# Regrouping TensorE's attention work and sharing half of w_in between two batches, in an attention and MLP kernel on one core

## The chip, the cores and the metric

The kernel runs on one core of a Trainium2 chip. The metric is the device time of one execution in microseconds (us), as the median of several executions. Before the change it is 1549.52 us (three runs, 1549.14 to 1550.99). The profiled execution: its span, from the first to the last instruction, is 1543.8. Profiles are used only to see where time goes.

Engines: TensorE (PE: matmuls; PEld: its weight loads), VectorE (DVE), ScalarE (ACT), GpSimd (POOL), SyncE (SP, which issues transfers). The granted clock is the share of TensorE's full clock that the profile shows for a stretch. A matmul of the program shows as two instructions in the profile, a transpose as one; each is called a pass here, and the counts (x8) are passes. An eviction is the instruction that takes a finished product out of its PSUM bank.

## The reference, cut to what matters

```python
# attention: batch 8, heads 12, sequence 448, head_dim 64, float32
q_n, k_n = rmsnorm(q, g_q), rmsnorm(k, g_k)       # x / sqrt(mean(x*x) + 1e-6) * g
attn = softmax(q_n @ k_n.T / 8)
x = (attn @ v).transpose(0, 2, 1, 3).reshape(3584, 768)
# then an MLP; w_in and w_out arrive as float64
h = x @ w_in                                       # 768 x 2048
out = (h * sigmoid(h)) @ w_out                     # 2048 x 768
```

## The kernel before

Attention goes by pairs of heads: 6 pairs a batch, 48 in all, numbered n. The keys' positions are cut into four chunks j of 112. The parts that matter, with cuts marked:

```python
def normalise(n):                    # two pairs ahead
    # ... cut: squares on ScalarE, sums and scaling on VectorE, power -0.5 on GpSimd
    for i, name in enumerate("qk"):
        # ... cut: factor = rms of this name
        nc.gpsimd.tensor_tensor(out=normal[name]..., in0=st[name], in1=factor..., op=ALU.mult)

def transpose(n, name):              # 4 TensorE transposes into the one bank "tr"
    # ... cut
    if name == "q":
        nc.scalar.copy(features[name], t)
    else:
        nc.vector.tensor_scalar_mul(out=features[name], in0=t, scalar1=gains)

def scores(half):                    # two chunks of keys, both heads: contraction over 64 rows
    for j in range(2 * half, 2 * half + 2):
        # ... cut: two matmuls into banks[:, h, :]
        nc.scalar.activation(e[j], banks[:, :, 0:S], AF.Exp)      # both heads at once

def weigh(n, half): ...              # "av": weights times values, 64 output columns
def add_up(half): ...                # VectorE: sums of the chunks' exps
def unload(n): ...                   # ScalarE: copy of av out of its bank
def divide(n):                       # "ones": sums of exp on TensorE, 64 output columns
    # ... cut
    nc.vector.reciprocal(out=r, in_=t)
    nc.vector.tensor_tensor(out=xT(*pairs[n]), in0=xU, in1=r, op=ALU.mult)
```

The MLP's products are work that TensorE does between the parts of attention. Two batches are a group, and a block of 256 of w_in's columns times the group takes seven products of half-size blocks (Strassen's way) instead of eight, with sums of blocks made on VectorE beforehand. In the first two batches the weights are still arriving, so batch 0 is multiplied plainly (`whole(0)`) and batch 1 in seven products on halves of its own 448 tokens, 224 columns each.

```python
for n, (b, hp) in enumerate(pairs):
    load(n + 2)
    scores(0)
    fill()                               # a quarter of the MLP work due in this pair
    if n > 0:
        divide(n - 1)
        # ... cut: beginning of the next group's products
    weigh(n, 0); scores(1); add_up(0)
    # ... cut: rounding of w_in (batch 1)
    fill()
    transpose(n + 1, "q"); weigh(n, 1); unload(n); add_up(1)
    # ... cut: rounding of w_in (batch 1); sums of w_in's blocks (batch 2)
    fill()
    transpose(n + 1, "k"); normalise(n + 2)
    # ... cut: rounding of w_in; end of a group: the rest of its products, sums of x
    fill()
divide(last)
# ... cut
for _ in halves_in(group, prepare_out):  # the last group, with nothing of attention beside it;
    pass                                 # prepare_out fetches hidden, opens and rounds w_out
# ... cut: the output stage, 14 products-of-seven over w_out
```

"Rounding" turns the float64 weights into float32 in steps: a load, an opening on ScalarE, then three instructions on VectorE and one on GpSimd.

## Time and profile before

The table reads TensorE's timeline at the sums of exp ("ones") of a pair, which come once a pair and so serve as marks. Work given in the second column lies between two marks.

| from the sums of pair | what runs | us | length |
|---|---|---|---|
| start to 0 | loads, first norms, first pair | 0 to 31.45 | 31.45 |
| 0 to 5 | batch 0: attention alone, rounding of w_in | to 92.36 | 60.9 |
| 5 to 23 | batches 1 to 3: attention and the first group's products | to 416.05 | 323.7 |
| 23 to 35 | batches 4 and 5, beside group 2 | to 653.61 | 237.6 |
| 35 to 47 | batches 6 and 7, beside group 3 | to 887.76 | 234.2 |
| 47 to end | last group, output stage | to 1543.8 | 656.0 |

One more view bears on the shared half of w_in: the list of what TensorE waited for between 246 and 400 us (engine, line, releaser: us in all, times, longest).

```profile
PE mm L434 <- DVE stage L408: 13.9, 9, 2.0
```

Nearly all of the 15.5 us of waiting in that stretch is for one kind of VectorE instruction, the eviction of a half-width product.

### The profile page before, as it was taken

Reading aid. Unit: us, or ns where it says so; the run is one execution under the profiler, and the core shown is the slowest. Engines: PE = TensorE matmul, PEld = TensorE weight load, DVE = VectorE, ACT = ScalarE, POOL = GpSimd, SP = SyncE. Lnnn points to the kernel's source line nnn. Section 1 sums busy time; section 2 is a strip of 40 time slices with the busy share of each in tenths; the row PEclk is TensorE's granted clock in tenths of the full one; section 3 lists DMA queues with packets and bytes.
Section 4 is the critical chain, followed back from the end, with each engine's and each line's share of the span. In section 5 each row is a group of like instructions: output and inputs, shape, how many; then the busy total and the mean of one; then the engine's idle time right before and its main releaser. Section 6 shows DMA issues by size and latency. Waiting matters only on the chain. (4 is left out here: it accounts for less than half of the span.)

```text
span 1543.8 us, 14413 instructions
## 1 busy us (share of the span) xinstructions
PE 1464.2 (95%) x5216; PEld 743.5 (48%) x5216; DVE 759.0 (49%) x970; ACT 525.3 (34%) x744; POOL 408.7 (26%) x300
## 2 busy tenths in 40 slices
PE   5789999899899999999999989999999999999998
PEld 2234444555444444344444344445555555555554
DVE  4988876655765555665555575662121112121221
ACT  4558865555544544544444423420000000000000
POOL 4555533333333323332333223330000000000000
PEclk9999999999899999999999999999999999999999
DMA  6344221121211211311131064442222222222220
GB/s 194 96 128 144 72 78 55 60 61 60 72 60 48 85 59 42 103 60 60 42 102 42 27 212 131 155 149 76 75 75 75 75 75 75 75 75 86 75 85 23
DMA packets 87924, 128.96 MB, mean 84 GB/s; under 512 B 5924, under 2 KB 70948, under 8 KB 87844
## 3 DMA queue, kind: packets, MB, share of 16 engines
q1 hardware_dynamic: 87520, 127.95, 26.5%
q8 instruction: 43, 0.70, 0.2%
q14 instruction: 37, 0.30, 0.1%
q10 hardware_dynamic: 324, 0.00, 0.0%
HBM read 87.56 MB, written 40.37 MB: 83 GB/s over the span
## 5 line engine op out<-in xcount | busy, mean ns | idle before, releaser
L434 PE MATMUL mm<-x,W 128*128 128x448 f32 (+1 forms) x768 | 283.4, 507 | 14.7 <-DVE stage L408 13.1
L335 POOL TENSOR_TENSOR rms<-rms,minus_half 112x16 f32<-112x16 f32 x48 | 141.0, 2937 | 408.4 <-DVE rms L332 394.9
L368 ACT ACTIVATE work<-sc 112x896 f32<-112x896 f32 x192 | 166.1, 914 | 203.3 <-PE sc L365 203.0
L434 PE MATMUL mm<-sums_x,W 128*128 128x448 f32 (+1 forms) x576 | 210.9, 500 | 14.7 <-DVE parts L408 9.3
L434 PEld LDWEIGHTS mm<-x,W 128*128 128x128 f32 x768 | 141.1, 192 | 148.6 <-issue 122.8
L446 POOL TENSOR_TENSOR parts<-parts 128x448 f32<-128x448 f32 (+2 forms) x46 | 49.2, 1069 | 582.1 <-DVE parts L408 581.8
L434 PE MATMUL mm<-W,work 128*128 128x384 f32 x588 | 197.6, 486 | 0.0
L365 PE MATMUL sc<-work 64*112 64x448 f32 x768 | 175.4, 577 | 17.8 <-DVE work L358 17.8
L399 DVE RECIPROCAL work<-tr 128x448 f32<-128x448 f32 x48 | 141.8, 2953 | 88.7 <-PE tr L398 88.7
L408 DVE TENSOR_TENSOR stage<-mm,parts 128x448 f32<-128x448 f32 (+2 forms) x121 | 67.7, 562 | 237.5 <-PE mm L434 101.2
L408 DVE TENSOR_TENSOR parts<-mm,parts 128x448 f32<-128x448 f32 (+2 forms) x92 | 51.6, 561 | 265.7 <-PE mm L434 256.5
L388 DVE TENSOR_TENSOR work<-work 112x896 f32<-112x896 f32 x144 | 169.0, 1174 | 12.1 <-ACT work L368 5.5
L377 PE MATMUL av<-work,rows 112*64 112x448 f32 x768 | 165.3, 552 | 3.6 <-ACT work L368 3.6
L434 PEld LDWEIGHTS mm<-sums_x,W 128*128 128x128 f32 x576 | 104.5, 190 | 105.6 <-issue 79.5
L434 PEld LDWEIGHTS mm<-W,work 128*128 128x128 f32 x588 | 111.7, 190 | 77.9
L365 PEld LDWEIGHTS sc<-work 64*112 64x112 f32 x768 | 62.4, 176 | 115.7 <-issue 63.8
L441 ACT COPY parts<-mm 128x448 f32<-128x448 f32 (+2 forms) x46 | 21.8, 474 | 268.9 <-PE mm L434 268.9
L434 PE MATMUL mm<-W,x 128*128 128x384 f32 x336 | 112.9, 486 | 0.0
L340 POOL TENSOR_TENSOR work<-rows,rms 112x512 f32<-112x512 f32 x96 | 100.6, 1069 | 3.8
L444 ACT COPY parts<-mm 128x448 f32<-128x448 f32 (+2 forms) x46 | 22.1, 481 | 221.9 <-PE mm L434 221.9
L377 PEld LDWEIGHTS av<-work,rows 112*64 112x64 f32 x768 | 50.6, 138 | 82.3 <-issue 53.5
L434 PEld LDWEIGHTS mm<-W,x 128*128 128x128 f32 x336 | 63.8, 190 | 44.5
(66 smaller groups left out, 1437.4 us busy)
## 6 DMA issues: line engine op xcount, KB each, us to landing
hidden<-stage SPq DMA_DIRECT2D x48, 448.0 KB, 2.5
work<-hidden SPq DMA_DIRECT2D x7, 2048.0 KB, 9.0
x<-hidden SPq DMA_DIRECT2D x7, 2048.0 KB, 9.0
W<-in_moe_w_in_dram SPq DMA_DIRECT2D x24, 512.0 KB, 4.1
rows<-in_moe_w_out_dram SPq DMA_DIRECT2D x32, 384.0 KB, 3.1
rows<-in_q_dram SPq DMA_DIRECT2D x48, 224.0 KB, 3.6
rows<-in_k_dram SPq DMA_DIRECT2D x48, 224.0 KB, 3.8
rows<-in_v_dram SPq DMA_DIRECT2D x48, 224.0 KB, 3.6
```

The costliest lines, as they stand in the source:

```text
L335: nc.gpsimd.tensor_tensor(out=flat, in0=flat, in1=minus_half[0:R].to_broadcast([R, 4 * J]), op=ALU.pow)
L340: nc.gpsimd.tensor_tensor(out=normal[name].rearrange("p j h d -> p h j d"), in0=st[name], in1=factor.to_broadcast([R, 2, J, D]), op=ALU.mult,)
L365: nc.tensor.matmul(banks[:, h, 0:S], kT[rows, ts(j, R)], qT[rows, :], start=True, stop=True)
L368: nc.scalar.activation(e[j], banks[:, :, 0:S], AF.Exp)
L377: nc.tensor.matmul(st["av"][ds(h * D, D), :], st["v"][:, h, j, :], e[j][:, h, :], start=(j == 0), stop=(j == J - 1),)
L388: nc.vector.tensor_tensor(out=es, in0=e[0] if j == 1 else es, in1=e[j], op=ALU.add)
L399: nc.vector.reciprocal(out=r, in_=t)
L408: nc.vector.tensor_tensor(out=out, in0=a, in1=b, op=ALU.add)
L434: nc.tensor.matmul(t, left(name, s), right(name, s), start=i == 0, stop=i == len(steps) - 1)
L441: nc.scalar.copy(p1, (yield from product("1")))
L444: nc.scalar.copy(p5, (yield from product("5")))
L446: nc.gpsimd.tensor_tensor(out=u2, in0=u2, in1=p5, op=ALU.add)
```

## The change

Its intent: (1) TensorE goes to attention twice a pair instead of four times. One visit is scores, av, transpose; the other is sums of exp, scores, av, transpose; a longer fill follows each. VectorE's other work (rounding, sums of weights) is dealt out between these points in single steps. (2) The keys aren't multiplied by their norm any more. They are transposed raw, and their factor is the scale operand of exp, which then has to be one instruction per head. (3) Half of w_in is multiplied plainly with batches 0 and 1, the other half with both as one group, so the half-width products vanish. (4) Small things at both ends: the first pair's norms go ahead, six matmuls of a new group go ahead of the last sums of the old one, the last group begins beside the last pair, and the last store is split.

```diff
+def normalise_rows(nc, z, rows, normal, squares, rms, minus_half, engine):
+    # ... cut: squares, sums, power as before; only q is multiplied, on `engine`
     # transpose(n, "k"), cut:
+            rows = state[n]["k"].rearrange("p h j d -> p j h d")
+            if n < 2 * z.NPAIR:
+                nc.scalar.activation(kT, t, AF.Copy, scale=gains)
+            else:
+                nc.vector.tensor_scalar_mul(out=kT, in0=t, scalar1=gains)
     # scores, cut:
-            nc.scalar.activation(e[j], banks[:, :, 0:S], AF.Exp)
+            for h in range(2):
+                nc.scalar.activation(
+                    e[j][:, h, :], banks[:, h, 0:S], AF.Exp, scale=rms[n % 4][:, 1, h, j : j + 1]
+                )
     # products of the first two batches:
     def first_two():
-        yield from whole(0)
+        yield from whole(1, early)
         for c in range(HW):
-            sum_x([1], c)
-        yield from halves_in([1])
+            sum_x([0, 1], c)
+        yield from halves_in([0, 1], late)
     # the loop, cut to its order:
+    for n in range(last + 2):
+        load(n + 3, "qk")
+        if n <= last:
+            scores(n, 0)
+        if n > 0:
+            weigh(n - 1, 1)
+            load(n + 1, "v")
+            add_up(2, 3)
+            unload(n - 1)
+        transpose(n + 1, "q")
+        if n == 0:
+            normalise(2)
+        if ends:
+            begin(halves_in([b - 2, b - 1], range(HF), prepare_out if b == z.B else plain),
+                  products, 4 * NPAIR - 1)
+        weights_in(n, 0)
+        fill(2 * HW if ends else None)
+        weights_in(n, 1)
+        if n > 0:
+            divide(n - 1)
+        if n <= last:
+            scores(n, 1)
+            weigh(n, 0)
+        transpose(n + 1, "k")
+        if n <= last:
+            add_up(1)
+        # ... cut: sums of x; at n = 6 and 12 the first products begin
+        weights_in(n, 2)
+        # ... cut: at a group's end, the rest of its products
+            fill()
+        weights_in(n, 3)
+        normalise(n + 3)
```

Further cuts: the loads of w_in keep a list of which raw buffer each needs and go as early as that is free; keys are loaded in another order of rows ("p j h d"); rings of buffers are dealt anew.

## The prediction

> **What bounds the kernel now.** I read part 1 of the page first, then the table of stages (TensorE's busy time in chosen stretches), the chain that ended last, and TensorE's timeline where the stretches show idle time.
>
> ```profile
> PE 1464.2 (95%) x5216; PEld 743.5 (48%) x5216; DVE 759.0 (49%) x970; ACT 525.3 (34%) x744; POOL 408.7 (26%) x300
> ```
>
> TensorE is busy for 1464 of 1543.8 us, every other engine for half the span or less. A gain can come only from less TensorE work or from its 80 idle microseconds. The stretches (start:end, length, TensorE busy, its instructions, granted clock, DMA share, GB/s) say where those are:
>
> ```profile
> 18.00:90.00 72.00, 56.96 (x260) 0.95 0.37 103
> ...
> 246.00:400.00 154.00, 138.49 (x684) 0.99 0.20 60
> ...
> 460.00:650.00 190.00, 186.69 (x693) 1.00 0.19 61
> ...
> 880.00:926.00 46.00, 39.03 (x108) 0.93 0.56 180
> 926.00:1029.00 103.00, 95.51 (x252) 1.00 0.41 134
> 1029.00:1544.00 515.00, 508.20 (x1574) 1.00 0.25 77
> ```
>
> Idle: about 16 us before the first scores at 18.6, 15.0 in batch 0 (attention with nothing to fill in), 15.5 while batch 1's products run on half-width operands, 3.3 in 190 us of the steady stage, 14.5 around the last group of two batches, 6.8 in the output stage, nearly all of it after the last matmul. The output stage isn't changed but for its last store, so a third of the span is fixed. Now one steady pair, in the chain (start, us, what, instructions):
>
> ```profile
> 785.68 1.65 PE av L377 x8
> 787.34 3.20 PE mm L434 x8
> 790.54 0.39 PE tr L354 x4
> 790.92 3.02 PE mm L434 x8
> 793.95 1.69 PE sc L365 x8
> 795.64 2.45 PE mm L434 x6
> 798.09 0.90 PE tr L398 x4
> 798.99 1.50 PE av L377 x8
> 800.50 1.69 PE sc L365 x8
> 802.19 3.20 PE mm L434 x8
> 805.39 0.39 PE tr L354 x4
> ```
>
> TensorE is never without work here, so only its own cost counts. Attention is 1.65+0.39+1.69+0.90+1.50+1.69+0.39 = 8.21 us. The four fills hold 30 passes (a matmul is two) in 11.87 us. In the last group the chain shows 25.09 us for 66 passes without a break, 0.380 each, so 30 should take 11.40: going in and out costs 0.47 us a pair. A fill of eight after av or sc takes 3.20, after a transpose 3.02; av after a transpose takes 1.65, after other matmuls 1.50.
>
> The half-width stage repeats this:
>
> ```profile
> 310.54 1.40 PE L434 MATMUL mm<-x,W 128*128 128x224 f32 x6
> 313.59 1.02 PE L434 MATMUL mm<-x,W 128*128 128x224 f32 x4 [1.65 <-DVE stage L408]
> ```
>
> Three products of 224 columns are over before VectorE has emptied the bank that the next needs.
>
> **What the Trainium skill says.** "TensorE: Matmul & The Clock Gate", section "HAM oscillation — how this bites in real kernels", warns of idle gaps over about 3.4 us, after which matmuls run at half clock. The trace agrees, even for shorter pauses: after the 2.39 us wait at 885.4 the next 12 passes take 7.16 us, where 12 later ones take 4.67. So the pauses between groups cost more than their length. "ScalarE: Activation LUTs", "What ACT_TABLE_LOAD costs", gives 1283 ns a load; the trace has 1283. "Perfetto Trace Analysis", "Optimizing Scalar/DVE Operations", says that each instruction carries a fixed access overhead, so that larger ones pay: the exp of 896 elements takes 914 ns, a copy of 448 out of PSUM 530, so two halves cost some 146 ns more than the whole. "DMA: Bandwidth & Descriptors", "Why small descriptors are slow (HBM only)", bears on the keys' new layout, whose rows are 256 B instead of 1 KB; no trace of before shows such a load. As keys are fetched three pairs ahead, I count nothing for it.
>
> **The change part by part.** I count to the last attention matmul (885.4 us now), then the rest.
>
> *Two visits.* Order per pair: scores, av, transpose, fill; sums of exp, scores, av, transpose, fill. Both fills follow a transpose (no entry cost seen), and both avs follow scores (1.50): attention 8.06, and 0.62 us less a pair. Fills run beside 42 pairs (batches 1 to 7): 42 x 0.62 = **-26 us**, all of it on the path.
>
> *Half of w_in shared.* Before, 168 half-width matmuls; after, 84 full ones: the same columns. Their 15.5 us of idle time should go, since a full product lasts 6 x 0.38 = 2.28 us against an eviction of 0.62. It is counted with the waits below.
>
> *Start.* The first pair's norms go ahead of the branch, and its keys are transposed without waiting for them. gains still waits for its DMA until 7.0; two reductions (0.67 each), the power (2.9 on GpSimd), the multiply on VectorE (about 0.7), transposes (0.98) and a copy (0.53) put the first scores at about 14.4 instead of 18.6. But the second pair's squares now stand behind that copy, and its query passes power and multiply again (15.3 to 20.6), so that the sums of exp of pair 0 come at about 31.7, as now (31.45).
>
> *Batch 0.* VectorE decides: it waits for sums of exp that wait for its own additions. A round after: reciprocal 2.95, multiply 0.65, three additions of 1.17, three rounding steps 1.5, reductions and scaling 1.45, and about 1.1 for TensorE's sums in between: 11.15 us. Now the sums of pairs 0 to 5 stand at 31.45 and 92.36, 12.2 apart. The keys' factor for the first two batches goes to ScalarE, and fewer waits lie in the round. Pair 5's sums at about 31.7 + 5 x 11.15 = 87.5: **-5 us**.
>
> *The other waits up to 885.4.* From pair 5's sums on, work now is 42 x 8.21 - 2 + 96 x 0.76 + 168 x 0.38 + 336 x 0.76 + 42 x 0.47 = 755 us; the trace takes 793, so 38 are waits and half-clock time: 15.5 above, about 5 at each change of group (402 to 416 and 641 to 655, idle plus slow clock), 4.4 between 90 and 210, the rest small. After, I allow 20: 2.5 at pair 12, whose first fill is empty; 3.5 at each of two changes of group (six matmuls go ahead, but the third product waits for the last sums of x); 2 in batch 1, where ScalarE needs about 13 of 14.9 us a pair; 0.2 a pair for the key transpose, which now stands 3.19 us of TensorE work (1.69+1.50) behind the sums, just as long as the reciprocal holds the bank (2.95 plus hand-over). **-18 us**.
>
> *The end.* Before the last group the first w_out tile still lands some 9.6 us after its load, and ScalarE's copies stand behind it; and the order of rounding and evictions on VectorE is unchanged, so the four waits of about 2.4 us stay. I give 1.5 for the overlap and 0.5 for the split last store: **-2 us**.
>
> *More work elsewhere.* ScalarE gets 192 x 0.146 = 28 us of exps, GpSimd loses 48 x 1.07 = 51. Neither is on the path.
>
> Sum: -26 - 5 - 18 - 2 = -51, so a span near 1493. The three timed runs are 5.7 us over the profiled span (1549.5 against 1543.8); with that, 1498.
>
> **The rivals.** (1) *The key transpose becomes a wait in every pair.* For it: there is no slack, and an eviction ahead of the reciprocal in VectorE's queue (0.62 us, or a wait for GpSimd's addition) passes on whole. Against: VectorE is busy about 60% of a pair, and the 5.5 us fill ahead gives it time. At 0.8 us a pair, 42 x 0.6 = 25 us are lost: 1523. (2) *ScalarE becomes the bound in batches 1 and 2*: smaller exps, table loads around every silu and two openings of w_in a pair fill 87% of the shorter pair. At 2 us a pair over 9 pairs: 1514. (3) *Everything goes well*: no wait at the transpose, 224-column stage and changes of group clean, the loads of the last group no longer seen: 12 to 20 us better, 1480. (4) *The saved time is taken elsewhere*, because TensorE's first matmuls after attention cost the same wherever they stand: half of the 26 us fails, 1511.
>
> **Range and chances.** All rivals but a combination stay ahead of 1518.5, the 2% line. The work taken away (26) and the half-width waits are read from traces directly; the 20 us of new waits is the weak term and could double. Hence 1498, 1477 to 1523; faster 0.86, within 2% 0.12, slower 0.02.
>
> **What would show it.** A steady pair in the chain should show two fills of about 14 or 16 passes, about 5.5 us each, and a period near 8.06 + 14.6 x 0.76 = 19.2 us instead of 20.1 to 20.85. The list of waits should show TensorE's transposes behind the reciprocal for under 15 us in all; over 30 means rival 1. Exp groups: 384 of about 530 ns. Pair 5's sums near 87.5, the stretch between 246 and 400 over 96% busy, and the last group's first products still pausing for w_out. The prediction is wrong if TensorE idles behind ScalarE in batches 1 to 3, or if fills keep their entry cost.

## The result and the profile after

The changed kernel takes 1541.99 us (median of four runs, 1540.31 to 1543.97) against 1549.33 us (four runs, 1547.24 to 1550.99). Executions over 1.5% slower than the fastest of the same kernel are left out of the means. Ratios here are the mean time of one kernel's runs over the mean of the other's runs of the same rounds, so not quite the ratio of the medians quoted: 0.9954, with a 95% interval of 0.9936 to 0.9972. That is "the same" at 2%, and 44 us above the prediction. Of these 44, 3.9 come from the way in which the prediction turned its span into a time: it added 5.7 us to its span, the distance from the profiled span to the median of other, slower executions. An execution's time is only 1.8 us over its own span, before (1545.57 and 1543.8) and after (1541.16 and 1539.4). For the same reason the spans differ by 4.4 us and the medians by 7.3.

The first line of the page, busy time by engine:

```profile
PE 1460.6 (95%) x5048; PEld 706.8 (46%) x5048; DVE 739.7 (48%) x939; ACT 562.9 (37%) x928; POOL 379.9 (25%) x243
```

TensorE's busy time fell by 3.6 us where 26 were to go, and its idle time is unchanged: 1539.4 - 1460.6 = 78.8 us, before 1543.8 - 1464.2 = 79.6. The stretches, placed at the same stages as those of before (start:end, length, TensorE busy, its instructions, granted clock, DMA share, GB/s):

```profile
14.00:90.00 76.00, 58.66 (x271) 0.96 0.44 122
240.00:400.00 160.00, 154.67 (x594) 1.00 0.22 67
444.00:638.00 194.00, 191.88 (x720) 1.00 0.23 68
863.00:912.00 49.00, 35.00 (x86) 0.79 0.49 161
912.00:1023.00 111.00, 99.63 (x256) 0.97 0.40 128
```

The stretch from 240 to 400 is now 97% busy, before 90%. But the beginning of the last group is idle for 14.0 of 49 us at a granted clock of 0.79, where it was idle for 7.0 of 46 at 0.93, and the rest of that group is idle for 11.4 us of 111, before 7.5 of 103. By the same marks as above:

| sums of pair | before | after | length before | length after |
|---|---|---|---|---|
| 0 | 31.45 | 34.91 | 31.45 | 34.91 |
| 5 | 92.36 | 91.85 | 60.9 | 56.9 |
| 23 | 416.05 | 401.32 | 323.7 | 309.5 |
| 35 | 653.61 | 637.51 | 237.6 | 236.2 |
| 47 | 887.76 | 871.18 | 234.2 | 233.7 |
| end | 1543.8 | 1539.4 | 656.0 | 668.2 |

From pair 23 on the marks of after have six matmuls (4.5 us) of the next group ahead of them. So the stage from 5 to 23 gained 18.7 us, the two steady stages almost nothing, and the end lost 16.7.

A steady pair in the chain that ended last (start, us, what, instructions):

```profile
437.18 1.65 PE av L412 x8
438.83 0.53 PE tr L377 x4
439.37 5.28 PE mm L472 x14
444.64 0.90 PE tr L433 x4
445.55 1.69 PE sc L396 x8
447.24 1.65 PE av L412 x8
448.89 0.53 PE tr L382 x4
449.43 5.28 PE mm L472 x14
454.70 1.69 PE sc L396 x8
```

(L433 is the sums of exp.) The shape is as intended: two visits, two fills of 14 passes without a wait. The pieces aren't: both transposes take 0.53 us instead of 0.39, and both avs 1.65. Attention costs 0.90 + 2 x 1.69 + 2 x 1.65 + 2 x 0.53 = 8.64 us a pair. Before it was 8.21, and 0.47 more in the fills, 8.68. The fills themselves are clean now, 5.28 / 14 = 0.377 a pass. The mean period from pair 24 to 34 is 19.76 us; 19.2 was predicted. Before it was 20.39 over the same pairs, but this is no gain of 0.6 a pair: the work of a group is spread otherwise over its pairs, and the whole stage from pair 23 to 35 is only 1.4 us shorter.

The last group, in TensorE's timeline (start, us, engine, line, operation, what, shapes, count, and in brackets the wait before it and its releaser):

```profile
863.78 4.78 PE L472 MATMUL mm<-x,W 128*128 128x448 f32 x12
871.18 1.76 PE L433 MATMUL tr<-work,ones 112*64 112x448 f32 x4 [2.62 <-DVE work L423]
881.99 3.35 PE L472 MATMUL mm<-sums_x,W 128*128 128x448 f32 x4 [9.05 <-ACT parts L479]
887.68 5.19 PE L472 MATMUL mm<-sums_x,W 128*128 128x448 f32 x8 [2.33 <-DVE sums_x L440]
```

In VectorE's timeline of the same kernel:

```profile
868.75 2.28 DVE L423 TENSOR_TENSOR work<-work 112x896 f32<-112x896 f32 x2
881.55 0.36 DVE L105 TENSOR_SCALAR x<-x 128x384 f32<-128x384 f32 x1 [10.52 <-ACT x L83]
882.82 2.95 DVE L434 RECIPROCAL work<-tr 128x448 f32<-128x448 f32 x1
```

In ScalarE's:

```profile
880.54 0.54 ACT L82 ACTIVATE rows<-rows 128x384 int32<-128x384 uint32 x1 [14.79 <-DMA rows<-in_moe_w_out_dram]
881.42 0.52 ACT L479 COPY parts<-mm 128x448 f32<-128x448 f32 x1
```

And in SyncE's, which issues the transfers (the second line spans several loads):

```profile
871.09 0.38 SPq L641 DMA_DIRECT2D work<-hidden  x1
871.52 23.78 SPq L67 DMA_DIRECT2D rows<-in_moe_w_out_dram  x7
```

Read the three from the bottom. The fetch of hidden is released when VectorE's last additions of exps end (871.03), because it lands in the buffer they use. The load of w_out stands behind the fetch in the queue and arrives at about 880.5. ScalarE's next instruction is the opening of those weights, so it stands for 14.79 us, and with it the copy of the first product (881.42), which is all that TensorE's third product waits for. VectorE's next instruction is the first rounding step, so it stands for 10.52 us, and with it the reciprocal of the last pair, whose operands were ready at about 873. Then TensorE waits again (2.33) for the sums of x that need that reciprocal.

### The profile page after: what moved, and what is told of

Same layout as the page of the kernel before. It is cut to its first block, busy times and chain, and to the rows that moved or that the text cites. A ratio compares the mean times of both kernels' runs of the same rounds, so it can differ in the third digit from the quotient of the medians.

```text
span 1539.4 us, 13964 instructions
## 1 busy us (share of the span) xinstructions
PE 1460.6 (95%) x5048; PEld 706.8 (46%) x5048; DVE 739.7 (48%) x939; ACT 562.9 (37%) x928; POOL 379.9 (25%) x243
## 3 DMA queue, kind: packets, MB, share of 16 engines
q1 hardware_dynamic: 118784, 127.95, 27.4%
## 4 chain that ended last, share of the span: by engine, by line
PE 86%; DVE 8%; DMA 3%; ACT 1%; issue 1%; POOL 0%; SPq 0%; ACTq 0%; DVEq 0%; POOLq 0%
PE mm L472 57%; PE sc L396 10%; PE av L412 9%; PE mm L506 5%; PE tr L433 3%; DVE work L423 2%; PE tr L382 2%; DMA rows<-in_moe_w_out_dram 2%; DVE sums_x L440 1%; PE tr L377 1%; DVE rms L292 1%; DMA rows<-in_k_dram 1%; DVE W L440 1%; DMA W<-in_moe_w_in_dram 0%; DVE x L440 0%
## 5 line engine op out<-in xcount | busy, mean ns | idle before, releaser
L401 ACT ACTIVATE work<-sc,rms 112x448 f32<-112x448 f32 x384 | 212.3, 635 | 227.0 <-PE sc L396 146.7
L472 PE MATMUL mm<-x,W 128*128 128x448 f32 x672 | 267.7, 542 | 1.3 <-DVE stage L443 0.9
L297 POOL TENSOR_TENSOR rms<-rms,minus_half 112x16 f32<-112x16 f32 x48 | 175.2, 3650 | 341.3 <-DVE rms L294 338.6
L472 PE MATMUL mm<-sums_x,W 128*128 128x448 f32 x504 | 212.6, 559 | 31.1 <-DVE parts L443 13.1
L484 POOL TENSOR_TENSOR parts<-parts 128x448 f32<-128x448 f32 (+1 forms) x42 | 45.6, 1085 | 611.0 <-DVE parts L443 611.0
L443 DVE TENSOR_TENSOR stage<-mm,parts 128x448 f32<-128x448 f32 (+1 forms) x109 | 66.1, 608 | 238.2 <-PE mm L472 144.9
L472 PEld LDWEIGHTS mm<-x,W 128*128 128x128 f32 x672 | 125.0, 191 | 117.1 <-issue 109.7
L443 DVE TENSOR_TENSOR parts<-mm,parts 128x448 f32<-128x448 f32 (+1 forms) x84 | 50.4, 600 | 254.6 <-PE mm L472 254.3
L479 ACT COPY parts<-mm 128x448 f32<-128x448 f32 (+1 forms) x42 | 21.8, 518 | 358.6 <-PE mm L472 358.6
L482 ACT COPY parts<-mm 128x448 f32<-128x448 f32 (+1 forms) x42 | 21.6, 515 | 250.7 <-PE mm L472 250.7
L472 PE MATMUL mm<-W,sums_x 128*128 128x384 f32 x252 | 84.7, 486 | 0.0
```

The source lines that it names most:

```text
L297: nc.gpsimd.tensor_tensor(out=flat, in0=flat, in1=minus_half[0 : z.R].to_broadcast([z.R, 4 * z.J]), op=ALU.pow)
L401: nc.scalar.activation(e[j][:, h, :], banks[:, h, 0:S], AF.Exp, scale=rms[n % 4][:, 1, h, j : j + 1])
L443: nc.vector.tensor_tensor(out=out, in0=a, in1=b, op=ALU.add)
L472: nc.tensor.matmul(t, left(name, s), right(name, s), start=i == 0, stop=i == len(steps) - 1)
L484: nc.gpsimd.tensor_tensor(out=u2, in0=u2, in1=p5, op=ALU.add)
```

## The experiments

Eight kernels, in two calls, each timed in five rounds beside the kernel before (medians of before: 1548.58 us in the first call, 1548.72 in the second). All results were correct. Only mended is past the 2% line; the other runs are "the same" as before at 2%, and what is said of them are smaller differences. A gain of a whole run is a difference of medians; after was timed earlier, beside a median of before of 1549.33. A gain at a mark is the mark's time in the one trace minus that in the other.

| run | edit against | median us (lowest to highest, runs) | ratio to before, 95% |
|---|---|---|---|
| after | - | 1541.99 (1540.31 to 1543.97, 4) | 0.9954 [0.9936, 0.9972] |
| av_first | after | 1545.13 (1543.38 to 1547.4, 6) | 0.9977 [0.9964, 0.999] |
| scores_split | after | 1558.83 (1557.63 to 1559.09, 5) | 1.0064 [1.0051, 1.0077] |
| loads_early | after | 1532.51 (1532.02 to 1533.19, 4) | 0.9893 [0.9878, 0.9908] |
| round_late | after | 1537.58 (1535.94 to 1540.25, 6) | 0.9929 [0.9916, 0.9942] |
| half_only | before | 1544.49 (1543.15 to 1544.86, 5) | 0.9974 [0.996, 0.9988] |
| keys_only | before | 1538.56 (1536.82 to 1539.46, 5) | 0.9933 [0.992, 0.9947] |
| fewer_loads | after | 1543.85 (1540.64 to 1545.67, 5) | 0.9964 [0.9951, 0.9978] |
| mended | after | 1509.06 (1506.14 to 1509.2, 5) | 0.974 [0.9727, 0.9753] |

### What a visit costs: av_first and scores_split

My theory after reading the two traces: what costs time is not a fill but a change of the array's shape. Matmuls of the MLP and transposes use the full array (F), scores use it halved in rows (R, a contraction over 64), av and the sums of exp halved in columns (C, 64 outputs). Per pair, with bars at the changes:

```
before        av | mm tr mm | sc | mm | ones av | sc | mm tr |            7 changes
after         mm | ones | sc | av | tr mm | sc | av | tr                  7 (ends on F as it began)
av_first      mm | ones av | sc | tr mm | sc | av | tr                    6
scores_split  mm | ones | sc | av | sc | tr mm | sc | av | tr             8
```

The rival: each visit has a cost of its own, so that the order inside it is indifferent.

```diff
 # av_first
         if n <= last:
-            scores(n, 1)
             weigh(n, 0)
+            scores(n, 1)
 # scores_split (scores takes which of its two chunks to do)
-            scores(n, 1)
+            scores(n, 1, (0,))
             weigh(n, 0)
+            scores(n, 1, (1,))
```

> The changed kernel with one pair's second visit reordered: sums of exp, av, scores instead of sums, scores, av. Nothing is added or taken away. Theory 1 (TensorE pays about 0.15 us at each change between full-array, row-halved and column-halved matmuls, and both kernels have seven changes a pair): six changes instead of seven, so the av after the sums falls from 1.65 to 1.50 us, a steady pair from 8.64 to about 8.49 us of attention, 42 to 48 pairs, 6 to 7 us less: about 1535. Theory 2 (the cost belongs to going in and out of a fill): no difference, 1542 within 1.

> The changed kernel with the second visit's two score chunks on either side of av: sums, scores, av, scores, transpose. Same instructions, still two visits. Theory 1 (cost per change of tile shape): nine changes instead of seven, about 0.3 us more a pair, 12 to 15 us over 42 to 48 pairs: about 1555. Theory 2 (cost per fill): 1542 within 1. A third possibility, that a later third score chunk delays something else, would show as waits of TensorE, not as longer entries.

In scores_split's expectation I had miscounted: it has eight changes, one more than after, as the sketch above shows.

Measured in the steady stage, av_first's second visit in the chain:

```profile
450.02 0.90 PE tr L433 x4
450.92 1.50 PE av L412 x8
452.43 1.69 PE sc L396 x8
454.12 0.53 PE tr L382 x4
```

The av behind the sums of exp, of the same shape, takes 1.50 and not 1.65. From pair 24 to pair 46 its marks move 3.3 us ahead of those of after: 3.3 / 22 = 0.15 us for one change fewer. For scores_split they fall 4.1 us behind, 0.19 for one more. So the theory of shapes holds in the steady stage with about 0.15 to 0.19 us a change, and the rival falls.

As a whole, av_first missed: 3 us slower than after and not 6 to 7 faster. Its loss lies in batch 0, 3.4 us, and in batch 1, 2.2. In the waits of TensorE between 36 and 96 us it has this line:

```profile
PE sc L396 <- ACT work L386: 8.0, 5, 1.6
```

The changed kernel has 3.9 us there, five times 0.8, and so has loads_early, whose batch 0 is the same program. (The length of batch 0 alone would not show it: loads_early's is 3.4 us longer than after's too, 60.3 against 56.9, at a lower granted clock.) With scores after av the exps come later, the copy of the next keys stands behind them on ScalarE in the first two batches, and batch 0 has no fill to cover it. The order is right only from batch 2 on, where VectorE makes that copy. scores_split lost 17 us in all; 4.1 are in the steady stage, some 4 in pairs 12 to 24, 2.6 in batch 1 (up to pair 12) and some 6 up to pair 5, partly half-clock time. Its 4 us in 12 pairs are more than 0.19 a pair; why was not looked into.

### The last group: loads_early and round_late

Theory: the load of w_out and the first rounding step, which went ahead of the last pair's reciprocal, make the loss. loads_early takes away the late load and leaves the order; round_late takes away the order on VectorE and leaves the load. (round_late's one more `yield` moves the first rounding, and what follows it in that block, by one product, not by two as its expectation says; that is enough to bring it behind the reciprocal.)

```diff
 # loads_early
         load(n + 3, "qk")
+        while n == last and rounder.load():
+            pass
 # round_late, in prepare_out
             rounder.open()
             yield
+            if m == 0 and rounder.rounded == 0:
+                yield
             rounder.round()
```

> The changed kernel with the first three w_out loads sent at the start of the last pair, ahead of the 2 MB fetch of hidden rows. Theory 3 (in the last group the first rounding step, which waits for that load, stands in VectorE's queue before the last pair's reciprocal and sums of x, and the opening before ScalarE's copy): the rounding no longer waits, the reciprocal starts near 872 instead of 882.8, the third product near 877 instead of 887.7: 10 to 12 us less, about 1531. Rival (the pause is VectorE's own work, eight sums of x, two additions, the reciprocal): at most 3 us less.

> The changed kernel with only the first rounding step moved two products later; the opening on ScalarE and all loads stay. Theory 3: the reciprocal and the sums of x are free of the load, but ScalarE's copy of the first product still stands behind the opening until about 882, so the third product starts near 882 instead of 887.7: about 6 us less, 1536. If only ScalarE's copy mattered: no difference. If only VectorE's order mattered: 10 to 12 us less.

loads_early gained 9.5 us (1541.99 to 1532.51), just under what was expected of it. From the last sums of exp to the end its trace takes 655.4 us, after's 668.2: 12.8 less. Although this trace reaches the last sums of exp 4.5 us later than that of after (875.67 against 871.18), its third product starts 4.6 us earlier, with no pause before it:

```profile
877.36 2.53 PE L472 MATMUL mm<-sums_x,W 128*128 128x448 f32 x4
882.34 5.01 PE L472 MATMUL mm<-sums_x,W 128*128 128x448 f32 x8 [2.44 <-DVE sums_x L440]
```

(The 887.7 of the expectation is the later part of the third product, which starts at 882.34 here.)

round_late gained 4.4 us, less than expected; from the last sums of exp to the end its trace is 6.1 us shorter (662.1). The reciprocal runs at 875.12, right behind the sums, but the third product still begins only at 883.86, after 8.77 us, as ScalarE's copy stands behind the opening as before. So both waits are real. Taking VectorE's alone away is worth some 6 us of the trace; with the load early, the first rounding and the opening no longer wait, so both go.

### Half of w_in alone: half_only

Theory: the shared half is what fills the stretch from 240 to 400. If so, it should give its gain without the rest. A rival is that it needs VectorE's work dealt out; one is that the gain came from the two visits.

```diff
 # half_only, in the kernel before, cut
     def first_two():
-        yield from whole(0)
+        yield from whole(1, range(z.NF // 2))
         for c in range(HW):
-            sum_x([1], c)
-        yield from halves_in([1])
+            sum_x([0, 1], c)
+        yield from halves_in([0, 1], ms=range(HF // 2, HF))
```

> The kernel before with one part of the change alone: the first two batches share seven products on half of w_in (84 products of 448 columns in place of 168 of 224), in the old order of four fills. Theory 4 (this part's use is that the 1.65 us waits of the 224-column products go): TensorE's waits for VectorE's evictions between batches 2 and 3 fall from 15.5 to under 4 us, 12 to 16 us less: 1533 to 1537, that is more than the whole change gave. Rival (the changed kernel's gain in batches 1 to 3 came from its two visits): at most 4 us less.

It gained 4 us. TensorE's waits between 90 and 450 us:

```profile
PE sc L365 <- DVE work L358: 10.6, 7, 3.5
...
PE mm L434 <- DVE stage L408: 2.8, 2, 2.6
```

The waits for evictions did go, as the theory says: 2.8 us where before has 13.9. But scores now wait longer for the copy of the keys, 10.6 us where before has 4.0. Of these, 3.5 and 2.0 end before the sums of pair 5, so they belong to batch 0; in batch 1 the wait is 4.8 us against 1.2. There VectorE's three rounding calls a pair meet a shorter pair. By the marks from pair 5 to 23 half_only gains 6.6 us of the 18.7 that the whole change gains there; 4 of these are lost again elsewhere, 2.3 of them behind the last sums of exp. So the gain has the size that the rival on record gave it (at most 4 us), but not for its reason, as the waits named by theory 4 did go. That the full gain needs VectorE's queue cleared too is my reading; no run shows it. My port spread the fills in its own way, so part of its loss may be the port's.

### The keys' factor alone: keys_only

Theory: this part gives nothing by itself, since neither GpSimd nor ScalarE is on the path.

```diff
 # keys_only, in the kernel before, cut
-        for i, name in enumerate("qk"):
+        for i, name in enumerate("q"):
             # ... multiply on GpSimd
-            nc.scalar.activation(e[j], banks[:, :, 0:S], AF.Exp)
+            for h in range(2):
+                nc.scalar.activation(
+                    e[j][:, h, :], banks[:, h, 0:S], AF.Exp, scale=state[n]["rms"][:, 1, h, j : j + 1]
+                )
```

> The kernel before with the keys' factor in exp's scale alone: 384 exps of 448 in place of 192 of 896, 48 GpSimd multiplies fewer, keys loaded in rows of 256 B and transposed raw. Theory: both engines have room, so the same within 3 us, 1546 to 1552. Rival (longer exp work reaches TensorE): av or scores waiting on ScalarE, 5 us or more slower.

It gained 10 us, more than the whole change, so the theory falls. The sums of pair 5 come 3.8 us earlier, 0.8 of it from the start; why was not looked into. The pairs 15 to 23 take about 1 us less each, and from pair 5 to 23 it gains 9.4 of the change's 18.7 us (half_only works on the same wait, so the two need not add up). GpSimd's timeline in the half-width stage shows what it does there; first before, then keys_only:

```profile
302.64 2.90 POOL L335 TENSOR_TENSOR rms<-rms,minus_half 112x16 f32<-112x16 f32 x1 [12.43 <-DVE rms L332]
305.62 2.04 POOL L340 TENSOR_TENSOR work<-rows,rms 112x512 f32<-112x512 f32 x2
307.62 0.66 POOL L446 TENSOR_TENSOR parts<-parts 128x224 f32<-128x224 f32 x1
```

```profile
316.36 2.91 POOL L337 TENSOR_TENSOR rms<-rms,minus_half 112x16 f32<-112x16 f32 x1 [12.42 <-DVE rms L334]
319.34 1.04 POOL L343 TENSOR_TENSOR work<-rows,rms 112x512 f32<-112x512 f32 x1
320.34 0.66 POOL L455 TENSOR_TENSOR parts<-parts 128x224 f32<-128x224 f32 x1
```

An addition of two products (the third line) is needed by the next eviction on VectorE. It stood behind the power and two multiplies, and now behind one. VectorE waited 5.46 us for GpSimd there before evicting, and now 4.46. TensorE's wait at the corresponding product fell from 1.65 us to 0.65. Between 90 and 450 us TensorE's waits for these evictions are as many as before, but half as long, where before has 13.9, 9, 2.0:

```profile
PE mm L443 <- DVE stage L417: 6.8, 9, 1.3
```

So GpSimd was on the path in this stage. The run changes the exps too, and no run takes away the multiply alone.

### The start: fewer_loads

Theory: the sums of pair 0 come late (34.91) because the second and third pair's rows arrive late behind 4 MB of w_in. The rival: another chain, through the second pair's power and multiply, is as long.

```diff
 # fewer_loads
-    while room.w_in.load():
-        pass
+    for _ in range(2):
+        room.w_in.load()
```

> The changed kernel with two pieces of w_in loaded at the start instead of eight; the rest follow pair by pair. Theory 5 (pair 2's queries and keys land only at 23.5 and 24.4 us because 4 MB of w_in stand ahead of them, and its norms stand ahead of the first additions in VectorE's queue): they land near 17, the sums of exp of pair 0 come near 32 instead of 34.9, about 3 us less: 1539. Half-clock spells of TensorE in batch 0 differ by up to 3 us from run to run, so this may drown. Rival (the loads aren't what the start waits for): the sums stay at 34.9.

The rows arrived early and the norms of pair 2 went right behind the copy of the first queries (22.28 us), but the sums stayed at 34.49, and the time is the same within the spread (1543.85 against 1541.99). In its chain stand the second pair's power and multiply on GpSimd (16.76 to 20.76), a transpose, scores at half clock (21.81, 2.75 us instead of 1.69), then openings and rounding. The rival holds: the loads aren't what the start waits for. That a second chain is about as long is read from the trace; no run shortens it.

### A version that mends what was found: mended

It takes loads_early and fewer_loads, puts av before scores from batch 2 on only, deals out the sums of a w_out chunk to two points, and spreads the first fills over all 12 points of batch 1.

```diff
 # mended, cut
+        while n == last and rounder.load():
+            pass
-            scores(n, 1)
-            weigh(n, 0)
+            if n < 2 * NPAIR:
+                scores(n, 1)
+                weigh(n, 0)
+            else:
+                weigh(n, 0)
+                scores(n, 1)
 # in prepare_out
+        yield
         if m % 2:
-            right_sums(*chunk_out(ORDER[m // 2]))
+            right_sums(*chunk_out(ORDER[m // 2]), (0, 1))
         yield
+        if m % 2:
+            right_sums(*chunk_out(ORDER[m // 2]), (2, 3))
-            begin(whole(0, early), len(early) * z.NW * S, 2 * NPAIR - 1)
+            begin(whole(0, early), len(early) * z.NW * S, 2 * NPAIR)
```

> The changed kernel with all repairs: w_out's first loads at the start of the last pair, av before the second scores from batch 2 on (six changes of tile shape a pair there), two pieces of w_in at the start, a w_out chunk's four sums dealt out two by two over two products, and batch 1's fill spread over one more place so that pair 12 has one. By the theories: 1542 less 10 (loads, measured), less 36 x 0.15 = 5 (shape changes), less 3 (start), less 8 to 12 (four waits of 3 us in the last group), less 3 to 5 (pair 12): 1508 to 1514. If a repair only moves a wait, less of it.

It takes 1509.06 us, inside what was expected and 2.6% faster than before. It is about 2.1% faster than the changed kernel (1509.06 / 1541.99 = 0.979, medians of different calls). In its span, 1507.3 us, the last attention matmul ends at 858.6 and the rest takes 648.7; after has 863.8 and 675.6. So 27 of the 32 us that it gains on after lie behind the last attention matmul. In TensorE's list of waits from 830 to 1040 us after has 26.2 us (9.1 for ScalarE's copy and 12.2 in the four waits of 3.0 among them); mended has 5.4:

```profile
PE mm L475 <- DVE sums_x L440: 3.2, 1, 3.2
PE tr L433 <- DVE work L423: 1.7, 1, 1.7
PE mm L475 <- DVE stage L443: 0.5, 3, 0.2
```

A steady visit in its chain:

```profile
500.42 0.90 PE tr L433 x4
501.32 1.50 PE av L412 x8
502.82 1.69 PE sc L396 x8
504.52 0.53 PE tr L382 x4
```

The sums of exp and av are of one shape, and av costs 1.50 again. What each edit gives in this combination was not run, but the marks tell where the terms of the expectation came true. The start gave none of its 3 us (the sums of pair 5 come at 94.47, in after at 91.85). From pair 5 to 12 it gained 3.6 us (3 to 5 expected for the spread fill), from pair 12 to 46 5.2 (5 expected for the shapes), and the end gave 26.9 where 18 to 22 were expected. So that the total fits is in part luck: the end made up for the start.

## Why the prediction was wrong

The span's sum can be set against the traces term by term. The last attention matmul ends at 885.4 before and 863.8 after.

| term of the prediction | predicted | measured | from |
|---|---|---|---|
| two visits | -26 | -2 | 42 x (8.64 - 8.68) |
| start and batch 0 | -5 | -0.5 | sums of pair 5: 92.36, 91.85 |
| other waits up to the last av | -18 | -19 | 863.8 - 885.4 = -21.6, less the two above |
| the end | -2 | +17 | 1543.8 - 885.4 = 658.4; 1539.4 - 863.8 = 675.6 |
| sum | -51 | -4.4 | span 1543.8, 1539.4 |

**Two visits: the step that failed by most.** "Both fills follow a transpose (no entry cost seen), and both avs follow scores (1.50)". The second half is a misreading. In the chain of before, av at 1.50 follows the sums of exp, not scores; behind scores it takes 1.65 in the changed kernel. And a transpose takes 0.39 only behind full-array work, 0.53 behind av. The cost of a fill's entry went out of the fills and came back in the transposes, because it belongs to the change of shape, of which there are seven a pair in both kernels. av_first and scores_split show it. The stages agree: from pair 23 to 47 the change gains 1.9 us in all. The Trainium skill has it: "TensorEngine Tiling (Array Packing)", under "Key Properties", says that changing the tiling mode drains the TensorE. I had not connected that with attention's 64-row and 64-column matmuls. Rival 4 named the effect (the saved time is taken elsewhere), but expected half of it and laid it to the first matmuls after attention.

**The end: the step that failed next, and the one that cost time.** "The order of rounding and evictions on VectorE is unchanged, so the four waits of about 2.4 us stay." The four waits stayed, at 3.0 and not 2.4 (12.2 us in all, before 9.3). But beginning the last group inside the loop, ahead of the last division, put the fetch, the load and the first rounding step in front of the reciprocal and ScalarE's copy. I had looked at what the early start lets TensorE do and not at what it puts into the queues of the other engines. loads_early and round_late show it: loads_early takes back 12.8 of the 17 us. The half-clock time after the pause enlarges it: 8 passes take 5.19 us at 887.68, against 3.02 at full clock.

**Start and batch 0: right in its mechanism, wrong in one mark.** First scores at 14.37 (14.4 predicted) and 11.1 us a pair in batch 0 (11.15) are right, but for the first of these pairs (12.54). But pair 0's sums come at 34.91 and not 31.7. The prediction saw the second query's power and multiply, but not that scores behind them run at half clock (the first take 3.33 us), nor the opening and rounding that stand behind them until 30.8. The same program can show pairs of 11.1 and of 12.7 us in batch 0, with a granted clock of 1.00 and 0.87 (loads_early from 47.43 and from 58.54 us); what decides between them is open.

**Other waits: right in size, partly for another cause.** Its 19 us are what is left over in the sum, so they hold whatever the other terms got wrong. The evictions of the half-width stage did cease to hold TensorE. But the reading "before VectorE has emptied the bank that the next needs" stopped one engine short: the eviction waited for GpSimd (keys_only). And half_only shows that the shared half alone brings 6.6 us of the 18.7 gained from pair 5 to 23. Around pair 12, which has no first fill, TensorE waits 3.3 us for a rounding step (2.5 were allowed for).

**More work elsewhere: the sizes were off, and for GpSimd "neither is on the path" is wrong.** Exps of 448 take 635 ns and not 530: 192 x (2 x 0.635 - 0.914) = 68 us more on ScalarE, not 28. From pair 24 to 34 keys_only stays 12.05 us ahead of before and from pair 36 to 46 10.28, so within the steady pairs nothing of that is on the path. GpSimd lost 28.8 us of busy time (408.7 to 379.9) and not 51, as its power took 3650 ns in the mean instead of 2937; why was not looked into. In the half-width stage of before GpSimd's work did hold TensorE up, as keys_only shows. "ScalarE: Activation LUTs", section "What ACT_TABLE_LOAD costs", says that each per-partition pointer operand adds about 93 ns to an activation, and the trace has 105 (635 - 530, against a plain copy; an exp of this size without the pointer was not run). The prediction should have used it.

**The rivals.** (1) Key transposes don't wait: TensorE's waits from 420 to 860 add up to 4 us in all. (2) In batch 1 the pairs take 15.46 us, which is 8.64 + 18 x 0.377 with no wait, so ScalarE bounds nothing. (3) didn't happen. (4) is true in direction, as told above.

The estimate had no term for a new wait at the end, and its rivals took away at most half of the gain of two visits, where nearly all of it failed. The check of the order of instructions was made for the loop and not for the iteration in which two stages overlap. One sentence of the prediction is also wrong in itself: rival 1 alone, at 1523, does not stay ahead of the line at 1518.5.

## What to carry to other kernels

Where matmuls of different tile shapes take turns, count the changes of shape over one period of the loop, and put those of one shape side by side; fewer visits by themselves saved nothing here. When work is begun earlier, read through each engine's queue at that place for what the early instructions wait for, because everything behind them waits too. And where an eviction is slow, follow its own wait to its releaser before saying which engine limits it.

## What the Trainium skill lacked or had wrong

- "TensorEngine Tiling (Array Packing)", "Key Properties": says that a change of mode drains the TensorE, but gives no size of that. Here a change costs about 0.15 us: av 1.65 against 1.50, transposes 0.53 against 0.39, and 0.15 to 0.19 us a pair for one change fewer or more. That a drain is the cause, no run shows.
- "TensorE: Matmul & The Clock Gate", "HAM oscillation — how this bites in real kernels": its rule of no gaps over about 3.4 us isn't enough here. Half clock followed a pause of 2.39 us before (12 passes in 7.16 us, later ones in 4.67), and of 2.33 and 2.44 us in after and loads_early, though these two came close on other pauses. It doesn't always follow: after 2.33 us before (at 926.84) and 3.02 in loads_early (at 910.67) the next 6 passes took 2.52. What decides is not shown.
- "DMA: Bandwidth & Descriptors", "Why small descriptors are slow (HBM only)": these runs don't contradict it, but the section gives no time for such a load. The keys in rows of 256 B landed in a median of 3.4 us, against 3.8 before with 1 KB rows, and the packets of the same 127.95 MB took 27.4% of the engines' time instead of 26.5%. With 224 KB loads fetched three pairs ahead no harm was seen.
